# Eight multiplications by a sign move from VectorE to GpSimd, each directly behind the product it reads

## The chip, the cores and the metric

The kernel runs on one core of a Trainium2 chip. The metric is the device time of one execution in microseconds (us). Before the change three executions took 1450.34, 1452.72 and 1458.42 us, a median of 1452.72. A core has five engines that run their own instruction lists in order and meet at semaphores: TensorE (PE, matmuls; PEld its weight loads), VectorE (DVE), ScalarE (ACT), GpSimd (POOL) and SyncE (SP), which here issues most DMAs.

## The reference

Three layers stand behind one another, all in float32, on 12480 tokens of width 128:

```python
# 1: a gated long convolution
h_filt = (np.maximum(pos_emb @ w1, 0) @ w2) * exp(-0.01 * pos)[:, None]
u = x * v
y = irfft(rfft(u, 2 * S) * rfft(h_filt, 2 * S))[:S]
a = x * y
# 2: a feed-forward block, 128 -> 2048 -> 128
r = np.maximum(a @ w_in, 0);  b = (r * r) @ w_out
# 3: a second one with a leaky slope per feature
h = b @ w_in2;  out = (np.maximum(h, 0) + alpha * np.minimum(h, 0)) @ w_out2
```

## The kernel before, in words

**The convolution** is a cyclic one of length 110 x 229 = 25190, and the Fourier transforms are matmuls against tables of cosines and sines: first over the axis of 110, then over that of 229. The 12480 tokens are packed, so that each of the 110 x 115 cells of a channel holds either the token at one position or the one at the mirrored position. The sum and the difference of the two positions, which the transform wants, then differ only in a sign of each cell: u = x * v is the one, and u times a table of +1 and -1 (`sig_sb`, 110 x 115) is the other.

The 128 channels go in 32 chunks of four (`DG` = 4, chunk number k). Chunk k has a pair of tiles, x and v, out of a ring of ten pairs (`NV` = 10) which lie in free parts of a large SBUF tile, G. Three steps prepare and use a chunk:

- `load` (L262): two DMAs on SP's queue bring x and v. They can start when the chunk ten places earlier has been used.
- `prep` (L270 and L209): GpSimd multiplies v by x into v (L270). A second multiplication takes that product times the sign table into x (L209, in the helper `signed`). This second one is on GpSimd for the first 16 chunks and for even k, and on VectorE for odd k from 17 on.
- `u_mm_a` and `u_mm_b`: the transforms. `u_mm_a` (L282) runs four matmuls on each of the two tiles, and ScalarE copies the results (L283). `u_mm_b` runs four matmuls (L290, L291, L292, L295), ScalarE copies the odd half (L294), and VectorE adds and subtracts (L298, two instructions) into U.

**The stages.** `u_stage(0)` takes chunks 0 to 15, interleaved with the transform of the filter (`r_stage`: matmuls L241, ScalarE L243, VectorE L247 and L248, a spill to HBM). `u_stage(1)` takes chunks 16 to 31, interleaved with the multiplication of the two spectra for the first half of the channels (`p_stage(0)`). In step k of either, the program emits `prep` for chunk k + 6, `load` for chunk k + 9, then `u_mm_a(k)`, and after it `u_mm_b(k-1)`.

**`p_stage`** has 14 passes for each half. A pass n makes the filter's spectrum by matmuls (two groups of eight, L341), and VectorE multiplies U by them into a tile T and into the PSUM tile `wide` (L346, in two pieces each), then combines the two (L355, twice). The closing additions and subtractions of the pass (`finish`, L325, four instructions in the first half) run on GpSimd and write back to U. T is a ring of two tiles, so L346 of pass n + 2 needs the closing additions of pass n to be done.

**What sets the order.** There is no scheduler: each engine's list stands in the order in which `run` draws from the two generators of a stage, with 32 units of `u_stage(1)` against 24 of `p_stage(0)`. So between two steps of `u_mm_a` TensorE has `u_mm_b` and, by turns, one or two of L341's groups. `u_mm_b` has two PSUM banks (`r_b`), one for the even half and one for the odd, so L291 of chunk k + 1 cannot write before VectorE's L298 of chunk k has read.

After these come `p_stage(1)` with the first half of the inverse transform (`b_stage`, L364), then the inverse transforms and the decoding of the weights, and from about 366 us on the two feed-forward blocks, in which TensorE runs three matmuls for each product (L576 to L578).

Of the kernel before, what the change touches and what calls it, by code (L numbers as in the profile page):

```python
# [31 lines left out]
DG = 4  # L32
NG = DH // DG
# [22 lines left out]
def kernel(  # L56
# [22 lines left out]
    nc = tc.nc  # L79
# [128 lines left out]
    def signed(eng, out, src, m):  # L208
        eng.tensor_tensor(out=out, in0=src, in1=sig_sb.unsqueeze(1).to_broadcast([NA, m, HB]), op=ALU.mult)  # L209

    def ar_stage():
        def turn(c):
            if c < F // 4:
                f = rv[:, 4 * c:4 * c + 4]
                signed(nc.vector if c < 2 else nc.gpsimd, f[:, :, 1], f[:, :, 0], 4)

        for c in range(4):
            turn(c)
        for c in range(F // 4):
            f0 = 4 * c  # L220
            p = [bank(r_any, HB, 4, K2) for s in range(2)]
            for s in range(2):
                for j in range(4):
                    nc.tensor.matmul(p[s][:, j], lhsT=rv[:, f0 + j, s], rhs=dfa)  # L224
            for s, copy in enumerate((nc.scalar.copy, nc.vector.tensor_copy)):
                copy(out=ar[s][:, :, f0:f0 + 4], in_=p[s].rearrange("p f k -> p k f"))
            turn(c + 4)
            load(min(4 + c // 3, n_first - 1))
            if c >= 10:
                prep((c - 10) // 2)  # L230
            yield
# [33 lines left out]
    def prep(n):  # L265
        while ready[0] <= min(n, 2 * NG - 1):
            k = ready[0]
            assert loaded[0] > k
            x, v = (t[:NA, :, 0:HB] for t in xv_ring[k % NV])
            nc.gpsimd.tensor_tensor(out=v, in0=v, in1=x, op=ALU.mult)  # L270
            signed(nc.vector if k >= NG and k % 2 else nc.gpsimd, x, v, DG)
            ready[0] += 1

    a_t = {}
# [25 lines left out]
    def u_stage(h):  # L300
        for k in range(h * NG, (h + 1) * NG + 1):
            if k < (h + 1) * NG:
                prep(k + NV - 4)
                load(k + NV - 1)
                u_mm_a(k)
                yield
            if k > h * NG:
                u_mm_b(k - 1)
                yield
# [583 lines left out]
```

## Time and profile before

| | |
|---|---|
| median of three runs | 1452.72 us |
| profiled execution | 1451.27 us, of which its span is 1449.5 us |
| TensorE busy | 1420.1 us (98%) |
| VectorE busy | 1115.2 us (77%) |
| ScalarE busy | 972.6 us (67%) |
| GpSimd busy | 994.5 us (69%) |
| mean granted TensorE clock | 0.994 of full speed |

The shares are means over stages with different limits, so a stage is read by itself: the busy time of each engine in a stretch says which engine fills it, and the timeline of an engine gives, in square brackets at the end of a row, how long it sat idle before that row and what released it. "DVE T L355" is VectorE's instruction of line 355 that wrote tile T. An engine's end of one row and the start of another's that waited for it lie next to each other in time.

### The profile page before, as it was taken

How to read it: one execution, taken by the hardware profiler on the slowest of the kernel's cores; microseconds unless marked ns; L12 is line 12 of the kernel's file. 1: busy time of each engine (PE TensorE's matmuls, PEld its weight loads, DVE VectorE, ACT ScalarE, POOL GpSimd, SP SyncE). 2: the span in 40 equal slices, each digit the busy share in tenths (PEclk: the TensorE clock that was granted, in tenths of full speed). 3: DMA queues.
4: the chain of work that ended last, by engine and by line, in shares of the span. 5: the costliest groups of instructions: out<-in, count | busy, mean ns of one | idle time of the engine just before them, and what ended most of it. 6: DMA issues, size and time to landing. Idle time of an engine off the chain costs nothing.

```text
span 1449.5 us, 22776 instructions
## 1 busy us (share of the span) xinstructions
PE 1420.1 (98%) x7598; PEld 1218.0 (84%) x7598; DVE 1115.2 (77%) x1802; ACT 972.6 (67%) x1843; POOL 994.5 (69%) x830
## 2 busy tenths in 40 slices
PE   9998889999999999999999999999999999999998
PEld 8998788989788888888888888888888888888887
DVE  4456699777787877777777777777777777778998
ACT  3443222441888777777777777777777777777776
POOL 4933556443777777777777777767777777776776
PEclk9999899999999999999999999999999999999999
DMA  8566213368300000000000000000000000000000
GB/s 201 166 188 176 66 53 118 79 183 248 124 23 1 1 8 8 9 1 8 8 9 8 8 1 8 8 8 8 1 8 8 8 8 8 1 8 9 15 8 19
DMA packets 59017, 66.19 MB, mean 46 GB/s; under 512 B 6336, under 2 KB 50963, under 8 KB 58771
## 3 DMA queue, kind: packets, MB, share of 16 engines
q1 hardware_dynamic: 57802, 60.62, 14.6%
q0 software_dynamic: 688, 3.93, 0.8%
q8 instruction: 59, 0.97, 0.3%
q14 instruction: 59, 0.48, 0.1%
q10 hardware_dynamic: 409, 0.19, 0.0%
HBM read 47.81 MB, written 16.92 MB: 45 GB/s over the span
## 4 chain that ended last, share of the span: by engine, by line
PE 89%; DVE 4%; issue 2%; POOL 2%; DMA 2%; ACT 1%; SPq 1%; POOLq 0%; DVEq 0%; ACTq 0%
PE bank L576 19%; PE bank L577 19%; PE bank L578 18%; PE pair L577 6%; PE pair L578 6%; PE pair L576 6%; PE bank L282 3%; PE bank L417 2%; PE bank L418 2%; PE bank L341 2%; PE bank L224 1%; PE pair L241 1%; DVE wide L346 1%; PE bank L364 1%; POOL G L325 1%
## 5 line engine op out<-in xcount | busy, mean ns | idle before, releaser
L629 POOL TENSOR_TENSOR g<-R,g 128x508 fp32r<-128x508 f32 (+1 forms) x598 | 776.0, 1318 | 274.8 <-ACT g L618 195.4
L611 DVE SCALAR_TENSOR_TENSOR R<-bank,e 128x508 f32<-128x508 f32 (+1 forms) x800 | 531.3, 674 | 171.2 <-POOL g L629 91.5
L618 ACT CAST g<-R 128x508 fp32r<-128x508 f32 (+1 forms) x800 | 466.6, 604 | 36.4 <-DVE R L611 32.6
L596 ACT ACTIVATE e<-bank 128x508 f32<-128x508 f32 (+1 forms) x400 | 234.9, 587 | 164.5 <-PE bank L578 163.2
L601 DVE TENSOR_SCALAR e<-bank,alpha 128x508 f32<-128x508 f32 (+1 forms) x266 | 195.3, 734 | 48.6 <-PE bank L578 48.5
L577 PE MATMUL pair<-g,w_o 128*128 128x508 f32 (+1 forms) x400 | 155.7, 389 | 0.6 <-POOL g L629 0.4
L629 DVE TENSOR_TENSOR g<-R,g 128x508 fp32r<-128x508 f32 (+1 forms) x202 | 155.5, 770 | 0.0
L578 PE MATMUL pair<-g,w_o 128*128 128x508 f32 (+1 forms) x400 | 155.1, 388 | 0.0
L576 PE MATMUL pair<-g,w_o 128*128 128x508 f32 (+1 forms) x400 | 154.1, 385 | 0.0
L576 PE MATMUL bank<-x,w_i 128*128 128x508 f32 (+1 forms) x400 | 153.9, 385 | 0.0
L577 PE MATMUL bank<-x,w_i 128*128 128x508 f32 (+1 forms) x400 | 153.3, 383 | 0.0
L578 PE MATMUL bank<-x,w_i 128*128 128x508 f32 (+1 forms) x400 | 153.2, 383 | 0.0
L577 PE MATMUL bank<-g,w_o0b 128*128 128x508 f32 (+1 forms) x350 | 136.8, 391 | 0.0
L576 PE MATMUL bank<-g,w_o0b 128*128 128x508 f32 (+1 forms) x350 | 136.0, 389 | 0.0
L578 PE MATMUL bank<-g,w_o0b 128*128 128x508 f32 (+1 forms) x350 | 135.3, 387 | 0.0
L598 ACT ACTIVATE e<-bank 128x508 f32<-128x508 f32 (+1 forms) x134 | 78.7, 587 | 32.9 <-PE bank L578 32.7
L599 ACT ACTIVATE e<-e,alpha 128x508 f32<-128x508 f32 (+1 forms) x134 | 95.5, 713 | 4.4
L576 PEld LDWEIGHTS bank<-x,w_i 128*128 128x128 f32 x400 | 75.3, 188 | 17.1 <-DVE R L611 1.0
L577 PEld LDWEIGHTS pair<-g,w_o 128*128 128x128 f32 x400 | 75.1, 188 | 15.4 <-DVE g L629 0.6
L578 PEld LDWEIGHTS pair<-g,w_o 128*128 128x128 f32 x400 | 75.0, 187 | 15.1
L577 PEld LDWEIGHTS bank<-x,w_i 128*128 128x128 f32 x400 | 75.0, 188 | 14.8
L578 PEld LDWEIGHTS bank<-x,w_i 128*128 128x128 f32 x400 | 75.0, 188 | 14.7
(126 smaller groups left out, 2530.0 us busy)
## 6 DMA issues: line engine op xcount, KB each, us to landing
r<-spill SPq DMA_DIRECT2D x22, 460.0 KB, 3.2
G<-in_xs_dram SPq DMA_DIRECT2D x32, 224.0 KB, 3.6
G<-in_vs_dram SPq DMA_DIRECT2D x32, 224.0 KB, 4.2
spill<-r SPq DMA_DIRECT2D x14, 460.0 KB, 3.0
out_dram<-R SPq DMA_DIRECT2D x24, 254.0 KB, 2.0
R<-in_xt_dram SPq DMA_DIRECT2D x27, 218.0 KB, 3.9
s_w<-in_moe_w_in_dram SPq DMA_DIRECT2D x16, 256.0 KB, 3.3
s_w<-in_moe_w_out_dram SPq DMA_DIRECT2D x16, 256.0 KB, 2.9
```

Source lines behind the costliest of these rows:

```text
L282: nc.tensor.matmul(p[:, d], lhsT=y[:, d], rhs=dfa)
L341: nc.tensor.matmul(H[:, :, s, q], lhsT=r[:, q, 2 * s + c], rhs=w2_sb[:, h * D:(h + 1) * D])
L576: nc.tensor.matmul(p, lhsT=wl, rhs=xh, start=first, stop=False)
L577: nc.tensor.matmul(p, lhsT=wh, rhs=xl, start=False, stop=False)
L578: nc.tensor.matmul(p, lhsT=wh, rhs=xh, start=False, stop=last)
L596: nc.scalar.activation(out=r, in_=p, func=ACTF.Relu)
L598: nc.scalar.activation(out=r, in_=p, func=ACTF.Relu, scale=-1.0)
L599: nc.scalar.activation(out=r, in_=r, func=ACTF.Copy, scale=alpha[:, t:t + 1])
L601: nc.vector.tensor_scalar(out=r, in0=p, scalar1=0.0, scalar2=alpha[:, t:t + 1], op0=ALU.min, op1=ALU.mult)
L611: nc.vector.scalar_tensor_tensor(out=g, in0=p, scalar=0.0, in1=r, op0=ALU.max, op1=op)
L618: nc.scalar.copy(out=gh, in_=g)
L629: eng.tensor_tensor(out=gl, in0=g, in1=gh.bitcast(F32), op=ALU.subtract)
```

## The change

The sign multiplication of every chunk is on GpSimd, directly behind the chunk's product. Eight instructions move: those of chunks 17, 19 and 21, which VectorE ran during `u_stage(0)`, and those of 23, 25, 27, 29 and 31, which it ran during `u_stage(1)`.

```diff
             x, v = (t[:NA, :, 0:HB] for t in xv_ring[k % NV])
             nc.gpsimd.tensor_tensor(out=v, in0=v, in1=x, op=ALU.mult)
-            signed(nc.vector if k >= NG and k % 2 else nc.gpsimd, x, v, DG)
+            signed(nc.gpsimd, x, v, DG)
             ready[0] += 1
```

TensorE's, ScalarE's and SyncE's lists keep their order. On VectorE the place shown is in `u_stage(1)` beside the passes of `p_stage(0)`; L346 and L355 are the multiplications and the combination of a pass (T_998 and T_999 are the two T tiles), L298 is the end of `u_mm_b`. Before:

```order
L298 TENSOR_TENSOR R_81<-bank_71,G 115x4x112 x2
L346 TENSOR_TENSOR wide_994<-G,bank_74 115x128
L346 TENSOR_TENSOR wide_994<-G,bank_74 115x896
L355 TENSOR_TENSOR T_999<-T_999,wide_994 115x128x4 x2
L209 TENSOR_TENSOR G<-G,sig_sb 110x4x115
L346 TENSOR_TENSOR T_998<-G,bank_73 115x128
L346 TENSOR_TENSOR T_998<-G,bank_73 115x896
```

The same place after the change:

```order
L298 TENSOR_TENSOR R_81<-bank_71,G 115x4x112 x2
L346 TENSOR_TENSOR wide_994<-G,bank_74 115x128
L346 TENSOR_TENSOR wide_994<-G,bank_74 115x896
L355 TENSOR_TENSOR T_999<-T_999,wide_994 115x128x4 x2
L346 TENSOR_TENSOR T_998<-G,bank_73 115x128
L346 TENSOR_TENSOR T_998<-G,bank_73 115x896
```

One row has gone from between L355 of one pass and L346 of the next; the same holds at the seven other places, and the only L209 left on VectorE are two early ones of `ar_stage`, which uses the same helper for the filter.

On GpSimd the same stretch, from the closing additions (L325) of the first pass on, where L270 is the product of a chunk and L209 its sign. Before:

```order
L325 TENSOR_TENSOR G<-T_998 115x8x2x4 x2
L325 TENSOR_TENSOR G<-T_998 115x56x2x4 x2
L270 TENSOR_TENSOR G<-G 110x4x115
L209 TENSOR_TENSOR G<-G,sig_sb 110x4x115
L325 TENSOR_TENSOR G<-T_999 115x8x2x4 x2
L325 TENSOR_TENSOR G<-T_999 115x56x2x4 x2
L270 TENSOR_TENSOR G<-G 110x4x115
```

After the change:

```order
L325 TENSOR_TENSOR G<-T_998 115x8x2x4 x2
L325 TENSOR_TENSOR G<-T_998 115x56x2x4 x2
L270 TENSOR_TENSOR G<-G 110x4x115
L209 TENSOR_TENSOR G<-G,sig_sb 110x4x115
L325 TENSOR_TENSOR G<-T_999 115x8x2x4 x2
L325 TENSOR_TENSOR G<-T_999 115x56x2x4 x2
L270 TENSOR_TENSOR G<-G 110x4x115
L209 TENSOR_TENSOR G<-G,sig_sb 110x4x115
```

A sign now stands behind the second of these products as well, ahead of the next pass's closing additions.

## Rows read from the trace of the kernel before

**Rows 1.** The page, part 1: busy us (share of the span) xinstructions
```profile
PE 1420.1 (98%) x7598; PEld 1218.0 (84%) x7598; DVE 1115.2 (77%) x1802; ACT 972.6 (67%) x1843; POOL 994.5 (69%) x830
```
**Rows 2.** Busy time by stretch: length, PE, PEld, DVE, ACT, POOL, clock, DMA share, GB/s
```profile
75.00:118.00 43.00, 43.00 (x350) 42.32 (x349) 23.45 (x55) 20.00 (x44) 15.53 (x14) 1.00 0.66 187
...
131.00:157.00 26.00, 20.19 (x147) 19.17 (x146) 17.00 (x29) 6.58 (x13) 15.23 (x19) 0.93 0.48 127
157.00:183.00 26.00, 21.57 (x147) 20.27 (x146) 17.38 (x29) 6.38 (x12) 15.31 (x20) 0.87 0.19 55
183.00:206.00 23.00, 23.00 (x188) 22.56 (x187) 20.51 (x35) 8.04 (x16) 9.74 (x15) 1.00 0.27 83
206.00:272.00 66.00, 59.93 (x525) 56.14 (x524) 64.54 (x79) 17.45 (x33) 42.87 (x41) 1.00 0.27 80
...
366.00:1442.00 1076.00, 1075.32 (x4764) 884.89 (x4763) 857.26 (x1340) 839.83 (x1546) 803.50 (x620) 1.00 0.03 11
```
**Rows 3.** Waits, 118 to 206 us: who for whom, total us, times, longest
```profile
POOL G L325 <- DVE T L355: 50.7, 10, 17.7
...
DVE G L209 <- POOL G L270: 15.4, 4, 4.1
...
PE bank L291 <- DVE R L298: 10.2, 4, 3.3
```
**Rows 4.** Timeline, VectorE: start, us, row [idle before <-releaser]
```profile
140.13 0.64 DVE L209 TENSOR_TENSOR G<-G,sig_sb 110x460 f32<-110x460 f32 x1 [4.00 <-POOL G L270]
```
**Rows 5.** Timeline, GpSimd, 136 to 178 us
```profile
136.20 2.77 POOL L325 TENSOR_TENSOR G<-T 115x64 f32<-115x64 f32 x4 [1.54 <-DVE T L355]
138.92 1.17 POOL L270 TENSOR_TENSOR G<-G 110x460 f32<-110x460 f32 x1
145.76 2.76 POOL L325 TENSOR_TENSOR G<-T 115x64 f32<-115x64 f32 x4 [5.67 <-DVE T L355]
148.47 1.17 POOL L270 TENSOR_TENSOR G<-G 110x460 f32<-110x460 f32 x1
149.72 1.16 POOL L209 TENSOR_TENSOR G<-G,sig_sb 110x460 f32<-110x460 f32 x1
150.83 1.16 POOL L270 TENSOR_TENSOR G<-G 110x460 f32<-110x460 f32 x1
...
176.59 1.17 POOL L270 TENSOR_TENSOR G<-G 110x460 f32<-110x460 f32 x1
```
**Rows 6.** Timeline, TensorE, 137 to 194 us
```profile
137.69 1.77 PE L282 MATMUL bank<-dfa,G 110*115 110x112 f32 x16
...
143.08 0.64 PE L291 MATMUL bank<-G,dfb 115*115 115x224 f32 x2 [3.24 <-DVE R L298]
...
144.31 1.76 PE L341 MATMUL bank<-w_sb,r 128*115 128x128 f32 x8
...
148.44 1.04 PE L341 MATMUL bank<-w_sb,r 128*115 128x128 f32 x8
...
184.31 1.77 PE L282 MATMUL bank<-dfa,G 110*115 110x112 f32 x16
...
189.19 1.77 PE L282 MATMUL bank<-dfa,G 110*115 110x112 f32 x16
...
193.19 1.77 PE L282 MATMUL bank<-dfa,G 110*115 110x112 f32 x16
```
**Rows 7.** Line 209: duration ns min/median/max, first and last start us, forms
```profile
L209 POOL TENSOR_TENSOR G<-G,sig_sb x38: 1075/1162/1527, 19.3 to 175.5; 110x460 f32<-110x460 f32 x38
...
L209 DVE TENSOR_TENSOR G<-G,sig_sb x10: 626/636/1515, 19.3 to 177.8; 110x460 f32<-110x460 f32 x10
```
**Rows 8.** Timeline, GpSimd, 187 to 191 us
```profile
187.76 2.78 POOL L325 TENSOR_TENSOR G<-T 115x64 f32<-115x64 f32 x4 [3.82 <-DVE T L355]
```
**Rows 9.** Timeline, VectorE, 193 to 196 us
```profile
193.82 1.28 DVE L346 TENSOR_TENSOR T<-G,bank 115x128 f32<-115x128 f32 x2
```
**Rows 10.** Timeline, SP's queue: the last load of a chunk
```profile
150.43 0.44 SPq L262 DMA_DIRECT2D G<-in_vs_dram  x1
```

## The prediction

> **What bounds the kernel now.** I read the page's busy line first [rows 1]: TensorE is busy for 98% of the span and VectorE for 77%, so an instruction taken from VectorE is worth something only where TensorE waits for VectorE. The busy time by stretch says where that is [rows 2]. From 183 to 206 us TensorE is busy for all of 23.00 us; in the two stretches before, with the same loop, for 20.19 and 21.57 of 26, and there its granted clock is 0.93 and 0.87. From 206 to 272 us VectorE is the full engine (64.54 of 66), and from 366 us on TensorE is again (1075.32 of 1076).
>
> Then the waits of the poor stretch [rows 3]. The largest, GpSimd's 50.7 us for VectorE's L355, is idle time of an engine with room and costs nothing by itself. Two others form a chain: VectorE waits four times, 15.4 us, at L209 for GpSimd's product, and TensorE waits four times, 10.2 us, at L291 for VectorE's L298. The timelines show how. GpSimd starts the closing additions of a pass at 136.20, when VectorE's L355 lets it, and the product of the odd chunk stands behind them, 138.92 to 140.09 [rows 5]. VectorE reached that chunk's sign 4.00 us before it could run, at 140.13 [rows 4]. Behind the sign are L346 of the next pass and L298, and for L298 TensorE sat idle 3.24 us, until 143.08 [rows 6]. GpSimd in turn idled 5.67 us until VectorE had finished that pass [rows 5]. So the two engines take turns instead of overlapping, though the sign's data isn't wanted for another six steps of the loop.
>
> **What goes.** VectorE loses eight signs. Of its ten L209 two belong to the filter at 19 us and stay. Five lie in this stretch, at 0.636 us each by the median [rows 7]: 3.2 us, together with the 15.4 us of waiting 18.6 us, the most that VectorE can give back. The three of chunks 17 to 21 lie in `u_stage(0)`, where TensorE is busy for 43.00 of 43 us and VectorE for 23.45 [rows 2]: nothing comes of them.
>
> TensorE sets the smaller bound. In the undisturbed part one step, from L282 to L282, is 4.88 us with two groups of L341 (184.31 to 189.19) and 4.00 with one (189.19 to 193.19) [rows 6]. The seven steps from 137.69 to 184.31 took 46.62 us. They are four short and three long ones, by the alternation of the two kinds; undisturbed they take 4 x 4.00 + 3 x 4.88 = 30.64. The loss is 46.62 - 30.64 = 16.0 us. It has two parts: the 10.2 us of idle time, and matmuls at the lower level of the clock. After the 3.24 us gap eight matmuls of L341 take 1.76 us, and at 148.44 they take 1.04 [rows 6]; the clock averages of the two stretches give 26 x 0.07 + 26 x 0.13 = 5.2 us [rows 2], and 10.2 + 5.2 = 15.4 agrees with 16.0. The clock part returns only because the gaps close.
>
> What is late next when L209 no longer waits? From 183 to 206 us VectorE runs the same loop without a sign, and TensorE is never starved there: VectorE has 20.51 us of work in 23 [rows 2]. That stretch is the model for the seven steps. So I count the whole of TensorE's loss, 16.0 us, and not the 18.6 us of VectorE.
>
> **What is added.** GpSimd gets eight signs of 1.162 us [rows 7], 9.3 us. For the first three there is room: 15.53 us busy of 43 [rows 2], and their chunks are used six steps later. For the other five the room must be counted. From product to product with a sign between is 150.83 - 148.47 = 2.36 us, the closing additions of a pass 2.77 [rows 5]. Four steps of the loop last 2 x 4.88 + 2 x 4.00 = 17.76 us and hold four chunks and three passes: 4 x 2.36 + 3 x 2.77 = 17.75 us. GpSimd is just full for as long as chunks are left. From the first pass's closing additions on there are eight chunks left, 24 to 31, among some seven passes: 8 x 2.36 + 7 x 2.77 = 38.3 us of work, in seven passes of 17.76 / 3 = 5.92, or 41.4 us. It fits with 3.1 us over, and only the queue's order can make a pass late.
>
> How late may it be? Behind a sign stand the closing additions, and for those waits L346 two passes on, which needs the T tile. In the undisturbed part the additions end at 187.76 + 2.78 = 190.54 [rows 8], and L346 takes the tile at 193.82 [rows 9]: 3.28 us of slack. Where two chunks stand together in GpSimd's list, the pass behind them has 4.72 + 2.77 = 7.49 us of queue against a period of 5.92, so it ends 1.6 us late, which the slack covers. If the slack is gone, what lies beyond it is charged in full to VectorE and so to TensorE.
>
> The data's other end has room as well. The last product runs at 176.59 [rows 5] and the last load was issued at 150.43 [rows 10]; even 16 us earlier the product stands 10 us behind its load, unless the load moves too. TensorE's use of a chunk comes six steps after its product was emitted, 3 x 4.88 + 3 x 4.00 = 26.6 us. TensorE gets a wait for GpSimd's sign where it had one for VectorE's, with the same six steps of lead. ScalarE's and SyncE's order doesn't change.
>
> A rule speaks against the change. The Trainium skill, GPSIMD Engine Reference, section "Engine selection", keeps elementwise work on VectorE, since two-input operations are about twice as slow on GpSimd. The trace agrees on the price, 1.162 against 0.636 us, a factor of 1.83 [rows 7]. By the rule taken as a verdict the eight would cost 8 x 0.526 = 4.2 us; by the trace they lie in GpSimd's idle time.
>
> **The sum.** 16.0 us less, nothing added: 1451.27 - 16.0 = 1435.3 us for an execution like the profiled one (span 1449.5, 1.8 us around it). The median of the runs shown is 1.45 us above that execution, so I put the forecast at 1436. Behind 206 us every stage waits only for work ahead of it on the same engines, so it is entered 16 us sooner and keeps its length.
>
> **The rivals.**
> First, GpSimd's fuller queue takes part of the gain back. For it: the 17.75 of 17.76 us. Against it: the surplus of 3.1 and the slack of 3.28. Its longest row of L209 took 1.527 us, not 1.162 [rows 7], a factor of 1.31. Were all its rows so long in this stretch, 38.3 becomes 50.2, which passes 41.4 + 3.3 = 44.7 by 5.5 us: 1441.5. The two engines reading SBUF at once would be a cause. The Trainium skill, SBUF — State Buffer, section "Who interferes with whom", has them share one pair of ports that either holds alone; the trace has a sign on GpSimd at 1.16 us and additions at 2.76 while VectorE works beside them, and shows no such loss in this stretch. I take up to 10 us for this rival: 1439 to 1446.
>
> Second, the wait changes only its name. VectorE no longer stops at L209, but stops as long at L346, because GpSimd's additions come after a product and a sign each time. For it: both engines lean on each other in one chain. Against it: the view of the waits has none of L346 for GpSimd in this stretch, and GpSimd itself waits for VectorE [rows 3]. It gives 1451 us. That the moved signs lie on the path at their price belongs here too: 1451.27 + 4.2 = 1455.5, near enough to no change.
>
> Third, slower: GpSimd becomes the bound of the seven steps. The mechanism is the one of the first rival, with rows so much longer beside a busier VectorE that T is always late. The gain is eaten when the work passes 44.7 + 16.0 = 60.7 us, that is at 60.7 / 38.3 = 1.58 times the rows shown. At twice the rows it is 76.6, and the time 1451.3 + 15.9 = 1467 us. Against it: no row of L209 is longer than 1.31 times the median [rows 7].
>
> **How the numbers follow.** Forecast 0.76, with a range of its own of 1432 to 1439; the queue's share 0.12, 1439 to 1446; no change 0.08; slower 0.04. The lower end is VectorE's bound, 1451.3 - 18.6 = 1432.7, rounded down. The range 1432 to 1446 holds the first two cases, and leaves out the last two and a little scatter of single runs, which lie up to 8 us apart. About 0.5%, 7 us, is what a measurement of this kernel can tell from no change: faster 0.88, same 0.08, slower 0.04.
>
> **What would show it.** Right: no L209 on VectorE after 22 us; TensorE's steps 4.00 and 4.88 us all the way, from its L282 of 137.69 on, with a clock of 1.00; the stage that VectorE fills begins at 190 instead of 206 us; the feed-forward blocks at 350 instead of 366 with their length unchanged. Wrong: L346 on VectorE with a wait for GpSimd's L325; L209 or L325 on GpSimd longer than 1.3 and 3.0 us; TensorE's L291 still waiting for L298; or L282 waiting for a sign of GpSimd, which would mean that six steps of lead are not enough.

## The result, and the profile after

| | before | after |
|---|---|---|
| median | 1452.96 us (4 runs, 1450.34 to 1458.42) | 1435.91 us (4 runs, 1434.86 to 1436.53) |
| span of the profiled execution | 1449.5 us | 1434.0 us |

The ratio is 0.988, with a 95% interval of 0.985 to 0.991. The forecast was 1436. The experiments below were timed beside further runs of the kernel before, whose medians were 1452.0 to 1452.9 us.

The busy time by stretch of the kernel after, with the columns of [rows 2], answers to those rows. The later borders are moved forward by 16 us:

```profile
75.00:118.00 43.00, 43.00 (x349) 42.33 (x348) 21.49 (x51) 20.31 (x44) 20.29 (x18) 1.00 0.66 190
...
131.00:157.00 26.00, 26.00 (x212) 25.50 (x212) 23.26 (x40) 9.14 (x18) 23.97 (x28) 1.00 0.53 146
157.00:183.00 26.00, 26.00 (x212) 25.50 (x211) 23.05 (x38) 9.49 (x18) 18.04 (x23) 1.00 0.30 92
...
190.00:256.00 66.00, 59.93 (x523) 56.11 (x522) 64.70 (x80) 17.32 (x32) 43.31 (x42) 1.00 0.27 80
...
350.00:1426.00 1076.00, 1075.32 (x4764) 883.81 (x4762) 856.94 (x1339) 839.47 (x1547) 803.59 (x620) 1.00 0.03 11
```

TensorE fills the two poor stretches (26.00 of 26 us, where it had 20.19 and 21.57) at a clock of 1.00. The stretch of `u_stage(0)` is as full as it was. The stretches behind have the same TensorE busy time in the same length, 16 us earlier.

The waits of the kernel after, from 118 to 190 us, answer to [rows 3]. Neither VectorE's L209 nor TensorE's L291 is among them any more:

```profile
POOL G L325 <- DVE T L355: 30.0, 6, 16.5
...
DVE wide L346 <- PE bank L341: 3.6, 4, 1.2
DVE R L298 <- ACT G L294: 3.5, 7, 0.7
```

The two rows of VectorE are waits for TensorE and ScalarE, 0.9 and 0.5 us each in the mean. TensorE's steps in the timeline of the kernel after, from the same L282 as in [rows 6]:

```profile
138.09 1.77 PE L282 MATMUL bank<-dfa,G 110*115 110x112 f32 x16
142.09 1.77 PE L282 MATMUL bank<-dfa,G 110*115 110x112 f32 x16
146.97 1.77 PE L282 MATMUL bank<-dfa,G 110*115 110x112 f32 x16
...
168.74 1.77 PE L282 MATMUL bank<-dfa,G 110*115 110x112 f32 x16
```

The steps are 4.00 and 4.88 us. The seven from 138.09 to 168.74 take 30.65 us, where they took 46.62; the sum of the prediction had 30.64 for them. GpSimd's timeline of the kernel after shows where the moved signs went, and answers to [rows 5]:

```profile
136.61 2.79 POOL L325 TENSOR_TENSOR G<-T 115x64 f32<-115x64 f32 x4 [1.55 <-DVE T L355]
...
141.72 2.77 POOL L325 TENSOR_TENSOR G<-T 115x64 f32<-115x64 f32 x4
144.44 1.17 POOL L270 TENSOR_TENSOR G<-G 110x460 f32<-110x460 f32 x1
145.69 1.16 POOL L209 TENSOR_TENSOR G<-G,sig_sb 110x460 f32<-110x460 f32 x1
146.82 1.16 POOL L270 TENSOR_TENSOR G<-G 110x460 f32<-110x460 f32 x1
148.06 1.17 POOL L209 TENSOR_TENSOR G<-G,sig_sb 110x460 f32<-110x460 f32 x1
149.19 2.77 POOL L325 TENSOR_TENSOR G<-T 115x64 f32<-115x64 f32 x4
...
172.19 2.77 POOL L325 TENSOR_TENSOR G<-T 115x64 f32<-115x64 f32 x4 [2.45 <-DVE T L355]
```

No row between the first and the last has an idle time in brackets, nor has one of those left out: GpSimd runs without a pause from 136.61 to 166.96 + 2.77 = 169.73. VectorE's timeline there has L355 of the pass whose additions stand at 149.19, and L346 two passes on:

```profile
146.25 1.29 DVE L355 TENSOR_TENSOR T<-T,wide 115x512 f32<-115x512 f32 x2
...
154.26 1.28 DVE L346 TENSOR_TENSOR T<-G,bank 115x128 f32<-115x128 f32 x2
```

L355 ends at 146.25 + 1.29 = 147.54, so the additions start 1.65 us late, as counted (1.6). They end at 149.19 + 2.77 = 151.96, and L346 takes the T tile at 154.26 without a wait: the slack covers the lateness with 2.3 us left.

### The profile page after: what moved, and what is told of

The parts are those of the page before. It is cut to its first block, busy times and chain, and to the rows that moved or that the text cites. A ratio compares the mean times of both kernels' runs of the same rounds, so it can differ in the third digit from the quotient of the medians.

```text
span 1434.0 us, 22784 instructions
## 1 busy us (share of the span) xinstructions
PE 1415.2 (99%) x7598; PEld 1213.7 (85%) x7598; DVE 1110.9 (77%) x1794; ACT 972.2 (68%) x1843; POOL 1003.9 (70%) x838
## 4 chain that ended last, share of the span: by engine, by line
PE 93%; DVE 4%; ACT 1%; issue 1%; DMA 1%; SPq 0%; POOL 0%; POOLq 0%; DVEq 0%; ACTq 0%
PE bank L578 19%; PE bank L577 19%; PE bank L576 19%; PE pair L576 6%; PE pair L577 6%; PE pair L578 6%; PE bank L282 3%; PE bank L341 2%; PE bank L417 2%; PE bank L418 2%; PE bank L224 1%; PE pair L241 1%; PE bank L364 1%; PE bank L290 1%; DVE wide L346 1%
## 5 line engine op out<-in xcount | busy, mean ns | idle before, releaser
L578 PEld LDWEIGHTS pair<-g,w_o 128*128 128x128 f32 x400 | 75.8, 189 | 16.9
L577 PEld LDWEIGHTS pair<-g,w_o 128*128 128x128 f32 x400 | 74.9, 187 | 16.8 <-DVE g L629 0.6
L576 PEld LDWEIGHTS bank<-x,w_i 128*128 128x128 f32 x400 | 75.2, 188 | 15.1 <-DVE R L611 1.0
L576 PEld LDWEIGHTS pair<-g,w_o 128*128 128x128 f32 x400 | 75.1, 188 | 14.3
L577 PEld LDWEIGHTS bank<-x,w_i 128*128 128x128 f32 x400 | 74.9, 187 | 14.5
```

What stands on the lines that cost most here:

```text
L576: nc.tensor.matmul(p, lhsT=wl, rhs=xh, start=first, stop=False)
L577: nc.tensor.matmul(p, lhsT=wh, rhs=xl, start=False, stop=False)
L578: nc.tensor.matmul(p, lhsT=wh, rhs=xh, start=False, stop=last)
```

## The experiments

**The question.** The prediction's theory is a wait: VectorE works its list in order, and the sign stood in it ahead of work that was wanted at once, although its operand came late from GpSimd and its result was needed only six steps later. A rival would give a change of the same size: VectorE is relieved of eight instructions, and of reading SBUF beside GpSimd.

All edits stand against the kernel after. **First, the signs stay on VectorE and only their place changes.**

```diff
+    held = []
     def prep(n):
+        while held and held[0][0] <= n - 2:
+            signed(nc.vector, *held.pop(0)[1:], DG)
...
-            signed(nc.gpsimd, x, v, DG)
+            if k >= NG and k % 2:
+                held.append((k, x, v))
+            else:
+                signed(nc.gpsimd, x, v, DG)
```

> The signs of the odd chunks 17 to 31 are on VectorE as in the kernel before, at the same kind of places in its list, but each belongs to the chunk two steps older, whose product has long been done. Theory of the wait (VectorE stands in order behind a product that GpSimd makes late): no wait of L209 for L270 is left, TensorE's steps are 4.00 and 4.88 us, and the time is 1436 us, up to 1438 since VectorE then has about 16.9 us of work in 17.8. Rival, the load (VectorE is relieved of eight instructions, or of reading SBUF beside GpSimd): nothing is relieved here, so 1452 us as before.

Measured: 1435.82 us (1434.84 to 1436.44), ratio to before 0.988 (0.987 to 0.990). With one step in place of two (`n - 1`):

> As in the run with the signs two steps later, but one step later only. Theory of the wait: a step of the loop is 4.00 to 4.88 us, the waits of before were 3.3 to 4.1 us, so they just vanish or leave a few tenths: 1436 to 1440 us. Rival, the load: 1452 us.

Measured: 1436.90 us (1435.66 to 1438.61), ratio 0.989 (0.988 to 0.991). In the busy time of the two-step kernel, the first of these, TensorE is as full as after the change (columns as in [rows 2]):

```profile
138.00:190.00 52.00, 51.97 (x421) 50.38 (x421) 49.12 (x81) 18.62 (x35) 36.48 (x44) 1.00 0.35 101
```

Every sign that the change moved is on VectorE here, and the gain is whole. So neither the relief of VectorE nor the engine that runs the sign is its cause; what counts is that the operand is there when VectorE's list comes to the sign.

**Then, parts of the change undone.** Chunks 17, 19 and 21 back on VectorE; then 23 to 31 instead; then 25 alone:

```diff
-            signed(nc.gpsimd, x, v, DG)
+            signed(nc.vector if k in (17, 19, 21) else nc.gpsimd, x, v, DG)
...
+            signed(nc.vector if k > NG + 6 and k % 2 else nc.gpsimd, x, v, DG)
...
+            signed(nc.vector if k == 25 else nc.gpsimd, x, v, DG)
```

> Only the signs of chunks 17, 19 and 21 are back on VectorE, in the stage where TensorE is busy all the time. Theory of the wait: 1436 us, the whole gain stays. Rival, the load: each of the eight moved signs is worth the same, so three eighths of 17 us are lost, 1442 us.

> Only the signs of chunks 23 to 31 are back on VectorE, in the stage beside the passes. Theory of the wait: all of the gain is lost, 1451 to 1453 us, with four waits of some 4 us at L209. Rival, the load: five eighths of 17 us are lost, 1446.5 us.

> Only the sign of chunk 25 is back on VectorE. Theory of the wait: VectorE waits there 4.0 us for the product, TensorE sits idle 3.2 us and runs at the lower level of its clock for some us after; the step took 8.17 us instead of 4.00 and the next 5.85 instead of 4.88, so 5.1 us are lost, 1441 us (1439 if the clock holds). Rival, each of the eight signs is worth the same: 17 / 8 = 2.1 us, 1438 us.

Measured: the three early ones 1435.30 us (1433.05 to 1436.73), ratio 0.988 (0.987 to 0.990), all of the gain kept. The five late ones 1454.01 us (1450.76 to 1457.41), ratio 1.001 (1.000 to 1.003), all of it lost (four of its five signs wait; in the kernel before, too, that of chunk 23 ran at 125.33 without a wait). Chunk 25 alone 1439.68 us (1436.66 to 1441.28), ratio 0.991 (0.990 to 0.993). The waits of the kernel with the five, 120 to 215 us, are those of [rows 3] again:

```profile
DVE G L209 <- POOL G L270: 16.2, 4, 4.1
...
PE bank L291 <- DVE R L298: 14.3, 5, 4.2
```

The kernel with chunk 25 alone shows one such wait by itself, on VectorE:

```profile
141.31 0.64 DVE L209 TENSOR_TENSOR G<-G,sig_sb 110x460 f32<-110x460 f32 x1 [4.01 <-POOL G L270]
```

and what TensorE made of it:

```profile
138.85 1.77 PE L282 MATMUL bank<-dfa,G 110*115 110x112 f32 x16
...
144.26 0.63 PE L291 MATMUL bank<-G,dfb 115*115 115x224 f32 x2 [3.25 <-DVE R L298]
...
145.49 1.04 PE L341 MATMUL bank<-w_sb,r 128*115 128x128 f32 x8
146.36 1.77 PE L282 MATMUL bank<-dfa,G 110*115 110x112 f32 x16
```

The step takes 146.36 - 138.85 = 7.51 us instead of 4.00: one sign at one place costs 3.5 us in this execution, against the 2.1 of an equal share and the 5.1 with the lower clock. The clock held here (eight matmuls of L341 in 1.04 us behind the gap), so what was expected with a held clock, 1439, is what the median of 1439.7 is nearest to. The times alone, from 1436.66 to 1441.28, would not tell the three expectations apart; the rows do. The profiled execution as a whole is the one of 1436.66 us, only 0.8 above the median of the kernel after, because it won time back later: from 256 to 350 us its granted clock was 1.00, where the profiled execution of the kernel after had 0.96. Against the profiled execution of the kernel with the three early signs (1433.05 us, mean clock 1.00 as here) it is 3.6 us longer.

**Product and sign both on VectorE**, for the odd chunks 23 to 31:

```diff
-            nc.gpsimd.tensor_tensor(out=v, in0=v, in1=x, op=ALU.mult)
-            signed(nc.gpsimd, x, v, DG)
+            eng = nc.vector if k > NG + 6 and k % 2 else nc.gpsimd
+            eng.tensor_tensor(out=v, in0=v, in1=x, op=ALU.mult)
+            signed(eng, x, v, DG)
```

> For the odd chunks 23 to 31 the product is on VectorE as well, in front of its sign; the rest is as after the change. VectorE has ten more instructions in the stage than after the change, five more than before. Theory of the wait (the cost was in waiting for the other engine, not in the place of the sign): nothing waits for a product, VectorE has 15.8 + 2.2 = 18.0 us of work in a period of 17.8, so about 1 us is lost, 1437 us. Rival, the load: VectorE is fuller than before the change, so 1452 us or more.

Measured: 1441.39 us (1438.97 to 1444.12), ratio 0.992 (0.991 to 0.994). The rival by load is far off, since VectorE has five instructions more in this stage than before the change and the kernel is 11 us faster. But 5.5 us are lost against the kernel after and not 1. VectorE's timeline of this kernel shows a cost that the expectation lacked (the edit shifts the lines by one, L271 is the product):

```profile
136.38 0.63 DVE L271 TENSOR_TENSOR G<-G 110x460 f32<-110x460 f32 x1
137.04 0.64 DVE L209 TENSOR_TENSOR G<-G,sig_sb 110x460 f32<-110x460 f32 x1
...
144.77 1.17 DVE L271 TENSOR_TENSOR G<-G 110x460 f32<-110x460 f32 x1
145.97 1.48 DVE L209 TENSOR_TENSOR G<-G,sig_sb 110x460 f32<-110x460 f32 x1
```

and GpSimd's beside it:

```profile
136.54 3.50 POOL L326 TENSOR_TENSOR G<-T 115x64 f32<-115x64 f32 x4 [1.55 <-DVE T L356]
142.67 2.77 POOL L326 TENSOR_TENSOR G<-T 115x64 f32<-115x64 f32 x4 [2.63 <-DVE T L356]
145.41 1.55 POOL L271 TENSOR_TENSOR G<-G 110x460 f32<-110x460 f32 x1
147.03 1.44 POOL L209 TENSOR_TENSOR G<-G,sig_sb 110x460 f32<-110x460 f32 x1
```

The pair of 136.38 begins 0.16 us before GpSimd's additions and takes 0.63 and 0.64 us; the additions take 3.50 us, not 2.77. The pair of 144.77 begins while GpSimd is already at work and takes 1.17 and 1.48, 1.38 us longer than the first. TensorE pays for it twice in this execution:

```profile
151.23 0.63 PE L292 MATMUL bank<-G,dfb 115*115 115x224 f32 x2 [2.09 <-DVE R L299]
...
171.46 0.64 PE L292 MATMUL bank<-G,dfb 115*115 115x224 f32 x2 [2.10 <-DVE R L299]
```

That is 4.2 us of idle time, in the fastest of the four executions (1438.97 us), where the medians differ by 5.5. The longer pair can account for 1.4 us of each gap; the other 0.7 would fit the fuller list, for which about 1 us in all was counted. No run separates the two.

**How much room has GpSimd?** The sign of chunks 24 to 31 runs twice, then three times, with the same result:

```diff
             signed(nc.gpsimd, x, v, DG)
+            if k >= 24:
+                signed(nc.gpsimd, x, v, DG)
```

> As after the change, but GpSimd runs the sign of each of the chunks 24 to 31 twice in a row (the second writes the same values again): 8 x 1.162 = 9.3 us of more work in its list. Theory of GpSimd's room (work that fits beside the passes is free, what goes beyond the surplus of 3.1 us and the slack of 3.28 us of a T tile is charged in full): 38.3 + 9.3 = 47.6 us against 44.7, so 3 us are lost, 1439 us. Rival, every microsecond of GpSimd's list is on the path by now: 1436 + 9.3 = 1445 us. Rival, GpSimd's list does not matter here: 1436 us.

> The same with each of these signs three times: 18.6 us of more work. Theory of GpSimd's room: 56.9 against 44.7 us, 12 us lost, 1448 us, with L346 on VectorE waiting for L325 on GpSimd. Rival, every microsecond is on the path: 1454.5 us. Rival, GpSimd's list does not matter: 1436 us.

Measured: twice 1442.07 us (1441.01 to 1447.38), ratio 0.994 (0.992 to 0.996); three times 1452.07 us (1450.20 to 1457.41), ratio 1.000 (0.999 to 1.002). The losses against 1435.9 are 6.2 and 16.2 us, where 3 and 12 were expected by GpSimd's room, and 9.3 and 18.6 by the rival that charges all. For the third sign the waits, 120 to 206 us, agree with the room (L326 and L347 are the closing additions and the multiplication into T here):

```profile
DVE T L347 <- POOL G L326: 16.4, 7, 5.4
...
PE bank L292 <- DVE R L299: 12.3, 2, 7.8
```

TensorE idles 12.3 us, against 12.2 counted. The rest of the 16.2 lies in the clock behind the two gaps: the two short steps that hold them take 10.43 (from 156.22) and 13.82 us (from 180.41) instead of 4.00, 16.3 us lost in all. For the second sign the profile is of the longest execution, 1447.38 us. TensorE's timeline shows one gap (this edit shifts the lines by two):

```profile
175.66 1.77 PE L284 MATMUL bank<-dfa,G 110*115 110x112 f32 x16
...
182.28 1.09 PE L293 MATMUL bank<-G,dfb 115*115 115x224 f32 x2 [4.46 <-DVE R L300]
...
184.65 1.92 PE L343 MATMUL bank<-w_sb,r 128*115 128x128 f32 x8
186.36 2.89 PE L284 MATMUL bank<-dfa,G 110*115 110x112 f32 x16
...
192.35 1.77 PE L284 MATMUL bank<-dfa,G 110*115 110x112 f32 x16
```

GpSimd's additions behind the last chunks, and VectorE's L348, which waits for them:

```profile
177.29 5.46 POOL L327 TENSOR_TENSOR G<-T 115x64 f32<-115x64 f32 x8
...
177.92 0.29 DVE L348 TENSOR_TENSOR T<-G,bank 115x128 f32<-115x128 f32 x1 [2.97 <-POOL G L327]
180.07 1.09 DVE L348 TENSOR_TENSOR T<-G,bank 115x896 f32<-115x896 f32 x1 [1.86 <-POOL G L327]
```

The gap is 4.46 us and not 2.9: the count took the surplus of 3.1 us as a mean over seven passes, but the last two chunks stand together in GpSimd's list (from 170.07 to 177.33) and the pass behind them comes late all at once, 4.8 us of waiting in one place. The two steps from 175.66 take 16.69 us instead of 8.88, so another 3.4 us are the clock's. One more execution of this kernel was profiled, to tell whether those near 1441 us have the gap without the clock's part:

> The kernel with the signs of chunks 24 to 31 twice, one look more. Its five executions lay at 1441.0, 1441.1, 1442.1, 1445.8 and 1447.4 us. If the spread is TensorE's clock after the one gap of 4.46 us, an execution near 1441 shows the same gap with a clock of 1.00 behind it, and one near 1446 shows 7.8 us lost there in two steps. If it is something else, the gap and what is lost behind it are the same in both.

Measured: 1446.26 us, with a gap of 4.48 us and the lower clock behind it. It was one of the longer executions again, so there is no profile of one near 1441 us, and how the median's 6.2 us divide stays open.

## Why the prediction was right

- **What goes.** The sum had one term, TensorE's loss of 16.0 us over seven steps. Undisturbed steps replaced all seven (30.65 against 30.64 us), and the span fell by 15.5: the kernel after entered the stage 0.4 us later in its execution (L282 of chunk 20 at 138.09, not 137.69). The medians lie 16.1 to 17.1 us apart, by the runs of the kernel before that one takes. The forecast was the sum's 1435.3 + 1.45 = 1436.7, rounded down to 1436, so that it lies within 0.1 us of the median is luck: the sum itself is 0.8 us above it.
- **The smaller bound was the right one.** VectorE's 18.6 us were not to be had: TensorE is at 26.00 of 26.
- **The three early signs** were counted at nothing, and undoing them costs nothing (1435.30). The five late ones carry all of it (1454.01).
- **The clock's part** of the term, put at 5.2 us, came back with the gaps closed (1.00 in place of 0.93 and 0.87). That it doesn't follow every gap is shown by chunk 25 alone.
- **What is added.** GpSimd's list was counted as just full and is (no pause from 136.61 to 169.73, 1.65 us late where 1.6 was counted). That such lateness turns into waits from there on is shown by the second and third sign; that it stays free up to there, by the kernel after.
- **The rivals.** A changed name of the wait, GpSimd as the bound, and moved signs at their price on the path would all have left L346 waiting for GpSimd or L291 for VectorE; neither wait is left. The first rival needed longer rows on GpSimd: between 129 and 190 us its signs take 1.16 to 1.17 us and its additions 2.75 to 2.79. The 1.527 us that it went by is a row of the filter's stage, among signs that run from 19.34 us while VectorE runs two of its own, from 19.29. The Trainium skill, GPSIMD Engine Reference, section "Engine selection", keeps elementwise work on VectorE and calls GpSimd about twice as slow for two inputs. The price agrees with the trace (a factor of 1.83), and here the slower engine had the time.
- **Sizes that were off** lie in the experiments: the cost of a full GpSimd list (6.2 for 3), by a mean where the order decides and by the clock; and product and sign on VectorE (5.5 for 1), by the row of 0.636 us, which doesn't hold for a pair that begins while GpSimd is at work.

One premise was left unnamed in the prediction: the first rival asked whether GpSimd would be slower beside VectorE. In the kernel before, the four signs that waited had their 0.64 us beside a GpSimd whose list the wait had emptied; a sign of VectorE that begins while GpSimd is at work takes 1.16 us or more in the rows shown. Of this kind is also VectorE's longest row in [rows 7], 1.515 us, in the filter's stage. After the change none of VectorE's rows in the stage is of this kind.

## What to carry to other kernels

An instruction whose operand comes late from another engine, and whose result is wanted late as well, should not stand in an in-order list ahead of work that is wanted at once: move it to the engine that makes the operand, or, as the two-step kernel shows with the same gain, put it some steps later in the list where it is. Look for it as a wait of one engine and idle time of its partner that alternate, and price it by the undisturbed steps of the same loop, not by the length of the instruction that moves. When a list is filled up for it, count the lateness of each item in its order; a surplus on the mean is not enough.

## What the runs showed of the hardware

**VectorE and GpSimd on SBUF.** A VectorE multiplication with both operands in SBUF takes 0.63 us alone, and 1.16 to 1.48 us in the rows shown where GpSimd had begun before it. Where VectorE began first, its row stays at 0.63 us and GpSimd's is the longer one. In the kernel with product and sign on VectorE, GpSimd's additions end at 142.67 + 2.77 = 145.44 and VectorE's product, started at 144.77, at 145.94, 0.50 us later. GpSimd's product ends at 145.41 + 1.55 = 146.96 and VectorE's sign at 147.45, 0.49 us later. GpSimd's product, begun at 145.41, in turn took 1.55 and not 1.16. So the later one waits for the other's end, instruction by instruction. The Trainium skill, SBUF — State Buffer, section "Who interferes with whom", describes such an exclusive lock on a pair of ports that the two share, and these rows agree with it. The two-step kernel has it too: on VectorE

```profile
136.30 0.63 DVE L209 TENSOR_TENSOR G<-G,sig_sb 110x460 f32<-110x460 f32 x1
144.02 1.16 DVE L209 TENSOR_TENSOR G<-G,sig_sb 110x460 f32<-110x460 f32 x1
```

and on GpSimd, where the product (L274) at 144.65, begun during VectorE's sign, is slowed as well:

```profile
141.92 2.76 POOL L332 TENSOR_TENSOR G<-T 115x64 f32<-115x64 f32 x4 [1.21 <-DVE T L362]
144.65 1.56 POOL L274 TENSOR_TENSOR G<-G 110x460 f32<-110x460 f32 x1
```

The sign of 136.30 begins 0.16 us before GpSimd's additions of 136.46, which take 3.12 us there. In that kernel VectorE had room for the half microsecond, and the time is the same. VectorE's L355, which reads one operand from PSUM, keeps its duration beside GpSimd. In the kernel after, five pairs of it, from 140.17 to 164.01, run while GpSimd works without a pause:

```profile
140.17 1.29 DVE L355 TENSOR_TENSOR T<-T,wide 115x512 f32<-115x512 f32 x2
```

All 56 rows of that kernel lie between 680 and 689 ns, as they did before the change (680 to 687), when GpSimd stood idle during every L355 from 128 to 206 us.

**TensorE's clock.** After a gap of 3.24 us in the kernel before, eight matmuls took 1.76 us [rows 6], with a granted clock of 0.54 from 144.3 to 146.1 us, so most of that time at the lower level of 1.2 GHz; after a gap of 3.25 us with chunk 25 alone they took 1.04 us, with a granted clock of 1.00, that is 2.4 GHz. The length of the gap doesn't settle it. With chunk 25 alone the gap cost 3.5 us, hardly more than itself; where the clock fell (0.50 from 182 to 186 us), behind the 4.46 us gap of the second sign, it cost 7.8.
